# Splitting the output and the last weight row of a DMA-bound decode kernel into quarters and halves

## The chip, the cores and the metric

The kernel runs on one core of one Trainium2 chip. The metric is device time in microseconds (us) of that core, for one execution. The kernel before takes 211.58 us (median of 3 runs, 211.49 to 211.81). The profile shows 209.7 us of them, from the first instruction to the last; this is called the span below. All times inside a trace are counted from the start of the span.

## The reference, cut to what matters

One decode step for four tokens (B = 4, D = 576): attention over a window of a cache, plus an MLP, plus the residuals.

```python
x  = A_x                                        # 4 x 1 x 576, bf16
xn = _layernorm(x)
# attention: 32 query heads, 16 K/V heads, Dh = 128, the last W = 2048 positions of the cache
q  = xn @ wq
p  = softmax(q k^T * Dh**-0.5)
A  = (p @ v) @ wo
# MLP, fed with xn: for one position the shifts of the mixer (w1, w2) leave only zeros
x1 = xn
Bm = x1 + _gelu(_layernorm(x1) @ w3) @ w4       # w3 is 576 x 4608, w4 is 4608 x 576
return x + A + Bm
```

The caches and the weights are read once: 87.17 MB. The last thing to be read is `w4`, and the last thing to be computed is its product, which is added in PSUM to everything that came before.

## The kernel before

`w4` stands in SBUF as 36 "rows": row u holds, on each of 128 partitions, one line of 576 bf16 numbers. Each row is one term of the sum over F = 4608. The kernel loads `w4` in six pieces, so that the matmuls of a piece can run under the load of the next one.

```python
NI = 2                     # the output's 576 columns in two halves
CW = D // NI
...
W4_PIECES = [0, NFH, NF - 12, NF - 6, NF - 2, NF - 1, NF]      # NF = 36, NFH = 18

def load_w4():
    t = wp.tile([P, NF, D], BF16, tag="w", name="w4_sb")
    for lo, hi in zip(W4_PIECES, W4_PIECES[1:]):
        e = lo // NFH
        src = B_w4[e * (F // 2):(e + 1) * (F // 2), :].rearrange("(p i) n -> p i n", i=NFH)
        nc.sync.dma_start(out=t[:, lo:hi, :], in_=src[:, lo - e * NFH:hi - e * NFH, :])
```

The four output rows are accumulated in PSUM in two halves of 288 columns. Half i lies in a bank of its own and on partitions 32i to 32i+3 (QD = 32), which is called column group i here. The two matmuls of a row run side by side: in the trace of this kernel they start 2 to 6 ns apart, and the next row 122 ns later at full clock.

```python
accs = [ps_acc.tile([P, CW], F32, name=f"acc{i}") for i in range(2)]

def acc_of(i):
    return accs[i * 2 // NI][i * QD:i * QD + B, :]

def acc_matmuls(terms):
    for lhsT, rhs in terms:
        for i in range(NI):
            nc.tensor.matmul(out=acc_of(i), lhsT=lhsT, rhs=rhs[:, i * CW:(i + 1) * CW],
                             start=False, stop=False, skip_group_check=True)
```

The end of the kernel is a row of small steps, one after the other: matmuls of the last piece, a copy of each half to bf16 (VectorE takes one, ScalarE the other), and the output DMA.

```python
    for lo, hi in pieces:
        mlp_out(lo, hi)                     # acc_matmuls of the rows of this piece

    fin = const.tile([B, D], out.dtype)
    for i in range(NI):
        dst = fin[:, i * CW:(i + 1) * CW]
        if i * 2 < NI:
            nc.vector.tensor_copy(out=dst, in_=acc_of(i))
        else:
            nc.scalar.activation(out=dst, in_=acc_of(i), func=ACT.Copy)
    nc.sync.dma_start(out=o2, in_=fin[:])
```

In the softmax, the sum of exponentials of a head is one f32 matmul (`dn`) and one reciprocal (`rd`) for each K/V head.

## Time and profile before

| | before |
|---|---|
| median of runs, us | 211.58 |
| span, us | 209.7 |
| bytes by the load queue, share of 16 DMA engines | 87.17 MB, 97.5% |
| mean granted TensorE clock | 0.91 |
| last byte of `w4` lands, us | 206.70 |
| output DMA is issued, us | 207.59 |

The word "tail" below means the last two rows of this table: from the landing of the last byte of `w4` to the issue of the output DMA, 0.89 us here.

How the views are read. In the slices, each digit is the busy share of one fortieth of the span, in tenths. A line of the timeline has start (us), duration (us), engine, source line, operation, output <- input, shape, number of instructions, and in brackets how long the engine had been idle and what ended that. A line of a chain has start, duration and what it was. A line of the windows has a stretch of time, its length, busy time (and number) of PE, PEld, DVE, ACT and POOL, then the granted clock, the DMA share and GB/s. The lines of the kernel before are shown in the prediction.

### The profile page before, as it was taken

What the parts mean: (1) busy time and instruction counts of PE and PEld (TensorE: products, weight loads), DVE (VectorE), ACT (ScalarE), POOL (GpSimd) and SP (SyncE); (2) the same over time, 40 slices, a digit from 0 to 9 for tenths busy, and PEclk for the clock granted to TensorE, in tenths of its full rate; (3) what the DMA queues carried; (4) which work ended last, traced back from release to release, by engine and by line L of the source; (5) the groups of instructions that cost most, each with busy time, mean ns of one, the idle gap of its engine ahead of it and who ended that gap; (6) DMA issues with size and microseconds to landing.
All of it is one profiled execution on the core that took longest, in us unless ns stands there. A gap on an engine that the chain in (4) does not pass through costs nothing.

```text
span 209.7 us, 2335 instructions
## 1 busy us (share of the span) xinstructions
PE 144.6 (69%) x955; PEld 57.5 (27%) x955; DVE 114.1 (54%) x165; ACT 34.0 (16%) x64; POOL 8.7 (4%) x31
## 2 busy tenths in 40 slices
PE   0358297699690039555999997589794846897694
PEld 0123032233130013222443332134231312342362
DVE  3611877885910083926519879166849391764200
ACT  7512201021120001111122211111111201113100
POOL 4610000000000000000002000000000000000000
PEclk9999579999888558999999999889999997999669
DMA  7999999999999999999999999999999999999992
GB/s 295 406 406 441 428 428 419 444 427 428 434 443 416 431 434 415 444 425 441 422 428 431 437 411 439 431 434 431 427 428 434 419 443 428 425 437 448 407 405 80
DMA packets 6650, 87.31 MB, mean 416 GB/s; under 512 B 744, under 2 KB 1008, under 8 KB 1648
## 3 DMA queue, kind: packets, MB, share of 16 engines
q1 hardware_dynamic: 6632, 87.17, 97.5%
q8 instruction: 7, 0.11, 0.2%
q14 instruction: 3, 0.02, 0.0%
q10 hardware_dynamic: 8, 0.00, 0.0%
HBM read 87.17 MB, written 0.00 MB: 416 GB/s over the span
## 4 chain that ended last, share of the span: by engine, by line
DMA 75%; PE 12%; DVE 10%; ACT 1%; issue 0%; SPq 0%; DVEq 0%; ACTq 0%
DMA kn<-in_A_k_cache_dram 30%; DMA vn<-in_A_v_cache_dram 24%; DMA w_sb<-in_B_w_dram 15%; DVE kt L222 7%; DMA wq_sb<-in_A_wq_dram 6%; PE S L335 3%; PE g_ps L452 2%; PE q_ps L279 2%; PE acc L181 1%; PE O L387 1%; DVE qz L311 1%; PE gT_ps L464 1%; DVE mx L341 1%; PE oT L400 1%; ACT q_sb L290 1%; PE S L357 0%
## 5 line engine op out<-in xcount | busy, mean ns | idle before, releaser
L335 PE MATMUL S<-kt,qz 128*128 128x512 bf16 x256 | 73.4, 413 | 34.0 <-DVE kt L222 33.8
L222 DVE STREAM_TRANSPOSE kt<-kn 128x2048 int32<-128x2048 int32 x32 | 73.4, 2297 | 28.3 <-DMA kn<-in_A_k_cache_dram 26.8
L335 PEld LDWEIGHTS <-qz 128*128 128x128 bf16 x256 | 23.4, 105 | 64.2 <-issue 46.2
L387 PE MATMUL O<-vn,PT 128*32 128x512 bf16 x256 | 22.6, 394 | 12.2 <-DMA vn<-in_A_v_cache_dram 12.2
L363 ACT ACTIVATE E<-S 128x512 bf16<-128x512 f32 x16 | 9.5, 597 | 96.6 <-PE S L357 96.6
L369 DVE STREAM_TRANSPOSE PT<-E 128x512 bf16<-128x512 bf16 x16 | 11.4, 710 | 13.8 <-ACT E L363 13.8
L394 ACT ACTIVATE O_sb<-O,rd 128x512 f32<-128x512 f32 x16 | 11.0, 686 | 37.0 <-PE O L387 37.0
L387 PEld LDWEIGHTS <-PT 128*32 128x32 bf16 x256 | 5.9, 94 | 32.6 <-issue 32.3
L410 DVE TENSOR_REDUCE on<-oT 128x8 bf16<-128x128 f32 x16 | 4.6, 287 | 18.7 <-PE oT L400 18.7
L400 PE MATMUL oT<-ident_w,O_sb 128*128 128x128 f32 x64 | 11.9, 314 | 0.2 <-ACT O_sb L394 0.2
L341 DVE TENSOR_REDUCE mx<-S 128x1 f32<-128x512 f32 x16 | 10.5, 658 | 1.2 <-PE S L335 1.1
L400 PEld LDWEIGHTS oT<-ident_w,O_sb 128*128 128x128 f32 x64 | 7.5, 153 | 4.4 <-issue 3.4
L357 PE MATMUL S<-nm,j_row 8*128 8x512 bf16 x16 | 6.5, 408 | 2.1 <-DVE nm L353 1.9
L373 PE MATMUL dn<-rs,same_j 128*128 128x1 f32 x32 | 6.2, 264 | 0.4 <-DVE g_x L470 0.4
L373 PEld LDWEIGHTS dn<-rs,same_j 128*128 128x128 f32 x32 | 5.0, 195 | 4.5 <-issue 3.8
L181 PE MATMUL acc<-wo_sb,op 128*4 128x288 bf16 x64 | 5.5, 324 | 1.0 <-DVE op L432 1.0
L323 PE MATMUL S<-negbig,ohT 4*128 4x512 bf16 x16 | 6.2, 385 | 0.0
L181 PE MATMUL acc<-w_sb,gT 128*4 128x288 bf16 x72 | 5.7, 315 | 0.4 <-DMA w_sb<-in_B_w_dram 0.4
L279 PE MATMUL q_ps<-wq_sb,xnT 128*32 128x512 bf16 x40 | 4.4, 625 | 2.2 <-DMA wq_sb<-in_A_wq_dram 2.2
L452 PE MATMUL g_ps<-w_sb,ln2T 128*32 128x512 bf16 (+1 forms) x50 | 4.9, 443 | 0.0
L602 DVE CAST fin<-acc 4x288 bf16<-4x288 f32 x1 | 0.4, 447 | 8.0 <-PE acc L181 8.0
L474 POOL TENSOR_TENSOR g_u<-g_x 128x144 f32<-128x144 f32 x1 | 0.4, 426 | 101.4 <-DVE g_x L470 101.4
(86 smaller groups left out, 74.4 us busy)
## 6 DMA issues: line engine op xcount, KB each, us to landing
kn<-in_A_k_cache_dram SPq DMA_DIRECT2D x16, 2048.0 KB, 24.5
vn<-in_A_v_cache_dram SPq DMA_DIRECT2D x16, 2048.0 KB, 26.5
wo_sb<-in_A_wo_dram SPq DMA_DIRECT2D x4, 1152.0 KB, 27.1
w_sb<-in_B_w_dram SPq DMA_DIRECT2D x1, 4608.0 KB, 33.2
wq_sb<-in_A_wq_dram SPq DMA_DIRECT2D x1, 4096.0 KB, 12.8
w_sb<-in_B_w_dram SPq DMA_DIRECT2D x1, 2592.0 KB, 33.1
w_sb<-in_B_w_dram SPq DMA_DIRECT2D x2, 864.0 KB, 34.5
w_sb<-in_B_w_dram SPq DMA_DIRECT2D x2, 576.0 KB, 32.5
```

Of the source, the lines that this page charges most:

```text
L181: nc.tensor.matmul(out=acc_of(i), lhsT=lhsT, rhs=rhs[:, i * CW:(i + 1) * CW], start=False, stop=False, skip_group_check=True)
L222: nc.vector.transpose(out=kt[:], in_=src)
L279: nc.tensor.matmul(out=q_ps[r][g * QD:(g + 1) * QD, :], lhsT=xnT[:, k, :], rhs=wq_sb[:, col:col + NW], start=(j == 0), stop=False, skip_gr ...
L335: nc.tensor.matmul(out=S_ps[h][:], lhsT=qz[:, z0:z0 + P], rhs=kt[:, ib, c0:c0 + SC, e:2 * QD:2].rearrange("p c k -> p (c k)"), start=False ...
L341: nc.vector.reduce_max(out=mx[:], in_=S_ps[h][:], axis=AX.X)
L363: nc.scalar.activation(out=E[h][:].rearrange("p c k -> p (c k)"), in_=S_ps.pop(h)[:], func=ACT.Exp, scale=scale, accum_out=rs[:])
L369: nc.vector.transpose(out=PT[h][:], in_=E.pop(h)[:])
L373: nc.tensor.matmul(out=dn[:], lhsT=same_j[:], rhs=st.pop(("rs", h))[:], start=True, stop=True)
L387: nc.tensor.matmul(out=O_ps[h][g * QD:(g + 1) * QD], lhsT=PT[h][:, c, :], rhs=vn[:, :, c, :], start=(s == 0), stop=False, skip_group_check ...
L394: nc.scalar.activation(out=O_sb[h][:], in_=O_ps.pop(h)[:], func=ACT.Copy, scale=st.pop(("rd", h))[:, 0:1])
L400: nc.tensor.transpose(out=oT[:, s, :], in_=o[:, s, :], identity=ident_w[:, s * NJ:s * NJ + P])
L452: nc.tensor.matmul(out=g_ps[g * QD:(g + 1) * QD], lhsT=ln2T[:, k, :], rhs=rhs, start=(j == 0), stop=False, skip_group_check=True)
```

## The change

Its intent: the last row's first half arrives before its second half. With the output in four quarters, quarters 0 and 1 are finished by the first half row and can be copied out while the second half row is still under way. So only two quarter copies, not two half copies, should lie after the last byte. The diff, cut to its core:

```diff
-    NI = 2
+    NI = 4
...
-    W4_PIECES = [0, NFH, NF - 12, NF - 6, NF - 2, NF - 1, NF]
+    W4_PIECES = [0, NFH, NF - 12, NF - 6, NF - 2, NF - 0.5, NF]
...                                        # load_w4 cuts the flattened (row, column) axis
+    late = {}
+
     def acc_of(i):
-        return accs[i * 2 // NI][i * QD:i * QD + B, :]
+        t = late.get(i, accs[i % 2])
+        return t[i * QD:i * QD + B, 0:CW]
...
     def mlp_out(lo, hi):
         w4 = w_tiles["w4"]
-        acc_matmuls([(gT[:, u, :], w4[:, u, :]) for u in range(lo, hi)])
+        for u in range(int(lo), NF):
+            quarters = [i for i in range(NI) if lo <= u + i / NI < hi]
+            acc_matmuls([(gT[:, u, :], w4[:, u, :])], quarters)
+
+    def copy_out(i):
+        dst = fin[:, i * CW:(i + 1) * CW]
+        if i % 2:
+            nc.scalar.activation(out=dst, in_=acc_of(i), func=ACT.Copy)
+        else:
+            nc.vector.tensor_copy(out=dst, in_=acc_of(i))
...                                        # after the last scaling of the loop
+    for i in (2, 3):
+        new = ps_s.tile([P, NW], F32, tag="S", name="late")
+        ...                                # acc_of(i) is copied to new, on DVE or ACT
+        late[i] = new
...
     for lo, hi in pieces:
         mlp_out(lo, hi)
+        for i in range(NI):
+            if lo <= NF - 1 + i / NI < hi:
+                copy_out(i)
```

Quarter i uses column group i, and so partitions 32i to 32i+3. Quarters 2 and 3 move late into the two score banks, which are free by then, so that each quarter has a bank of its own. Besides, the denominators of two heads are summed by one matmul and inverted by one reciprocal.

More of the change, by code (lines that the diff above doesn't have):

```diff
@@ L138, in load_w4 @@
         for lo, hi in zip(W4_PIECES, W4_PIECES[1:]):
-            e = lo // NFH
-            src = B_w4[e * (F // 2):(e + 1) * (F // 2), :].rearrange("(p i) n -> p i n", i=NFH)
-            nc.sync.dma_start(out=t[:, lo:hi, :], in_=src[:, lo - e * NFH:hi - e * NFH, :])
+            e = int(lo) // NFH
+            src = B_w4[e * (F // 2):(e + 1) * (F // 2), :].rearrange("(p i) n -> p (i n)", i=NFH)
+            lo, hi, cut = int(lo * D), int(hi * D), e * NFH * D
+            nc.sync.dma_start(out=t[:].rearrange("p i n -> p (i n)")[:, lo:hi], in_=src[:, lo - cut:hi - cut])
         w_tiles["w4"] = t
@@ L172, with acc_matmuls @@
         nc.vector.memset(acc[:], 0.0)
+    late = {}
     def acc_of(i):
-        return accs[i * 2 // NI][i * QD:i * QD + B, :]
-    def acc_matmuls(terms):
+        t = late.get(i, accs[i % 2])
+        return t[i * QD:i * QD + B, 0:CW]
+    def acc_matmuls(terms, quarters=range(NI)):
         for lhsT, rhs in terms:
-            for i in range(NI):
+            for i in quarters:
                 nc.tensor.matmul(out=acc_of(i), lhsT=lhsT, rhs=rhs[:, i * CW:(i + 1) * CW],
@@ L361, in sm_exp @@
         E[h] = ptp.tile([P, SC, QD], BF16, tag="e", name="E", bufs=1)
-        rs = small.tile([P, 1], F32, tag="rs", bufs=3)
+        if h % 2 == 0:
+            st["rs"] = small.tile([P, 2], F32, tag="rs", name="rs", bufs=3)
         nc.scalar.activation(out=E[h][:].rearrange("p c k -> p (c k)"), in_=S_ps.pop(h)[:], func=ACT.Exp, scale=scale,
-                             accum_out=rs[:])
-        st["rs", h] = rs
+                             accum_out=st["rs"][:, h % 2:h % 2 + 1])
     def sm_turn(h):
@@ L371, in sm_den @@
     def sm_den(h):
-        dn = ps_m.tile([P, 1], F32, tag="m", name="dn")
-        nc.tensor.matmul(out=dn[:], lhsT=same_j[:], rhs=st.pop(("rs", h))[:], start=True, stop=True)
-        st["dn", h] = dn
-    def sm_rec(h):
-        rd = small.tile([P, 1], F32, tag="rd", bufs=4)
-        nc.vector.reciprocal(out=rd[:], in_=st.pop(("dn", h))[:])
-        st["rd", h] = rd
+        if h % 2 == 0:
+            return
+        dn = ps_m.tile([P, 2], F32, tag="m", name="dn")
+        nc.tensor.matmul(out=dn[:], lhsT=same_j[:], rhs=st.pop("rs")[:], start=True, stop=True)
+        st["dn"] = dn
+    def sm_rec(h):
+        if h % 2 == 0:
+            return
+        rd = small.tile([P, 2], F32, tag="rd", bufs=4)
+        nc.vector.reciprocal(out=rd[:], in_=st.pop("dn")[:])
+        for k in range(2):
+            st["rd", h - 1 + k] = rd[:, k:k + 1]
     def pv(h, s):
@@ L393, in o_scale @@
         O_sb[h] = bigp.tile([P, NSL, Dh], F32, tag="big", name="O_sb")
-        nc.scalar.activation(out=O_sb[h][:], in_=O_ps.pop(h)[:], func=ACT.Copy, scale=st.pop(("rd", h))[:, 0:1])
+        nc.scalar.activation(out=O_sb[h][:], in_=O_ps.pop(h)[:], func=ACT.Copy, scale=st.pop(("rd", h)))
     def o_turn(h):
@@ L586 @@
     o_scale(hl)
+    for i in (2, 3):
+        new = ps_s.tile([P, NW], F32, tag="S", name="late")
+        if i % 2:
+            nc.scalar.activation(out=new[i * QD:i * QD + B, 0:CW], in_=acc_of(i), func=ACT.Copy)
+        else:
+            nc.vector.tensor_copy(out=new[i * QD:i * QD + B, 0:CW], in_=acc_of(i))
+        late[i] = new
     o_turn(hl - 1)
@@ L594 @@
     o_proj(hl)
+    fin = const.tile([B, D], out.dtype)
     for lo, hi in pieces:
         mlp_out(lo, hi)
-    fin = const.tile([B, D], out.dtype)
-    for i in range(NI):
-        dst = fin[:, i * CW:(i + 1) * CW]
-        if i * 2 < NI:
-            nc.vector.tensor_copy(out=dst, in_=acc_of(i))
-        else:
-            nc.scalar.activation(out=dst, in_=acc_of(i), func=ACT.Copy)
+        for i in range(NI):
+            if lo <= NF - 1 + i / NI < hi:
+                copy_out(i)
     nc.sync.dma_start(out=o2, in_=fin[:])
```

## The prediction

Passages of the prediction are cut, marked where they stood: figures and rules of the hardware that it did not take from a trace. Its sum is as recorded, 211.58 - 0.12 = 211.46 us, but the sources of three of its terms are among the cuts. Those terms stand because the trace of the changed kernel has since shown them: 0.226 us for a matmul of 144 columns at full clock (222 to 226 ns there), and 150 and 120 ns less for a copy of half the columns on DVE and ACT (447 to 295 ns and 401 to 281 ns, so 152 and 120). Rival B's reckoning came to +0.5 us, 212.1.

> **What bounds the kernel now.** I read the slices of the page first, then the chain that ended last, then the timeline of the last microseconds, because the change touches almost nothing else.
>
> ```profile
> DMA  7999999999999999999999999999999999999992
> GB/s 295 406 406 441 428 428 419 444 427 428 434 443 416 431 434 415 444 425 441 422 428 431 437 411 439 431 434 431 427 428 434 419 443 428 425 437 448 407 405 80
> q1 hardware_dynamic: 6632, 87.17, 97.5%
> ```
>
> In every slice but the first and the last the 16 DMA engines are at least 90% busy; they move 87.17 MB and are occupied for 97.5% of the span. The change moves the same bytes, so some 206 us out of 209.7 are fixed. Only what follows the last byte can be saved. The chain, from the last V load on:
>
> ```profile
> 174.85 31.13 DMA w_sb<-in_B_w_dram
> 205.98 0.04 issue
> 206.03 1.05 PE acc L181 x12
> 207.07 0.44 DVE fin L602
> ```
>
> This seems to give 1.05 us of matmuls to win. It does not, as the timeline around 207 shows:
>
> ```profile
> 206.74 0.29 PE L181 MATMUL acc<-w_sb,gT 128*4 128x288 bf16 x2
> 207.06 0.45 DVE L602 CAST fin<-acc 4x288 bf16<-4x288 f32 x1 [7.98 <-PE acc L181]
> 207.10 0.40 ACT L604 ACTIVATE fin<-acc 4x288 bf16<-4x288 f32 x1 [10.85 <-PE acc L181]
> 207.59 0.35 SPq L605 DMA_DIRECT2D out_dram<-fin  x1
> ```
>
> The last two matmuls (row 35 of w4) start at 206.74. The trace's records of landings give the reason: the six pieces of w4 are complete at 200.48, 202.46, 204.59, 205.98, 206.33 and 206.70. PE started the last row 0.04 us after its data; it had no backlog. So the tail is: last byte 206.70, +0.04 to the matmul, +0.29 matmul, +0.03 to the copy, +0.45 copy, +0.08 to the output DMA, then 2.14 us of output and end of program, which the change leaves alone. From last byte to output DMA there are 0.89 us, and only the matmul and the copy in it shrink with the column count.
>
> [...] with four column groups, 8 matmuls of 512 columns take 0.61 us[...]; their starts (trace records) are 3 ns apart inside a group of four.
>
> ```profile
> 180.19 0.12 PEld L387 LDWEIGHTS <-PT 128*32 128x32 bf16 x8 [0.44 <-issue]
> 180.19 0.61 PE L387 MATMUL O<-vn,PT 128*32 128x512 bf16 x8
> 180.73 0.36 PE L419 MATMUL R<-on,sel_wo 128*128 128x32 bf16 x8
> ```
>
> The third line is the narrow case in one group: 8 in 0.36 us, starts 25 ns apart[...].
>
> **The change part by part.**
>
> *Four column groups instead of two.* Each of the 36 rows of w4 and the 8 rows of each of four output projections now needs 4 weight loads and 4 matmuls of 144 columns. The order of instructions on PE has 266 more: 68 rows with 4 extra each is 272, 2 more for the first sum, 8 fewer for the denominators. Before, a row takes 122 ns at full clock and 240 ns at half (starts in the trace)[...]: both groups run together. Four groups at 144 columns should take half, about 62 and 120 ns. This lies under the DMA either way: PE waits for pieces already (0.36 us before 206.03). Worth 0 at the end.
>
> *Loads.* The last two pieces of 1152 B per partition become 1728 B and 576 B. Packets of 1152, 4608 and 6912 B take 51, 178 and 264 ns in the trace, which fits 6 ns + 0.0374 ns per byte; 1728 + 576 B cost 71 + 28 = 99 ns against 2 x 51 = 102. Same number of packets. So the last byte still lands at 206.70, and the larger piece, three quarters of the 0.72 us between 205.98 and 206.70, at 206.52. Worth 0 by itself.
>
> *Quarters 0 and 1.* Rows 30 to 33 start at 206.03 and need 0.25 us. Row 34 starts at 206.56, row 35 of quarters 0 and 1 at 206.62, and they are done at 206.62 + 0.226 = 206.85. Copies of 4x144: DVE [...]447 - 150 = 297 ns; ACT 401 - 120 = 281 ns. With the gaps of before (34 and 66 ns) they run from 206.88 to 207.18 on DVE and 206.91 to 207.19 on ACT.
>
> *Quarters 2 and 3.* The last half row starts at 206.74 and is ready at 206.74 + 0.226 = 206.97, so the second pair of copies could start at 207.00. But DVE and ACT are still in the first pair: "under the load" there are only 0.18 us between the landings, and a copy alone takes 0.3. Consecutive instructions that do not depend on each other overlap by some 80 to 90 ns on DVE:
>
> ```profile
> 86.80 0.23 DVE L343 TENSOR_SCALAR dm<-sel_g,mx 128x16 bf16<-128x16 bf16 x1
> 86.94 0.16 DVE L378 RECIPROCAL rd<-dn 128x1 f32<-128x1 f32 x1
> ```
>
> (0.23 us long, next start after 0.14). So the second copies start at about 207.09 and end at 207.39 (DVE) and 207.38 (ACT). The output DMA is issued at 207.39 + 0.08 = 207.47 against 207.59: 0.12 us less.
>
> *Moves of quarters 2 and 3 into the score banks.* One more copy each, on DVE after the last reciprocal (about 193.0, when it idles 3.16 us) and on ACT after the last scaling (ends 196.25). The first matmul that needs them is at 199.14. Hidden.
>
> *Denominators in pairs.* Eight pairs of f32 matmuls of 0.38 us on PE and eight reciprocals of 0.16 us on DVE go. For even heads the scaling on ACT now waits for the reciprocal of the same turn, behind the maximum on DVE: about 2 us later (180.85 to 182.91 in the turn I looked at). Its reader, the transposes at 184.89, comes later still. Loads are issued some 24 us ahead of landing, so none of this reaches the DMA. In the tail head 14's scaling moves from 192.55 to some 193.05; its transposes start at 195.39. Worth 0.
>
> **The sum:** 211.58 - 0.12 = 211.46 us.
>
> **The rivals.**
>
> *A. The copies of quarters 0 and 1 are fully hidden.* Then the end is 206.97 + 0.03 + 0.30 = 207.30, issue 207.38: 0.21 us gained, 211.37. For it: that is the intent. Against: 0.18 us between the two landings.
>
> *B. PE falls behind.* [...] Against: the 3 ns and 25 ns starts above. I give it one in twenty.
>
> *C. The clock falls.* Twice as fast, PE idles more, and the clock is granted by windows:
>
> ```profile
> 192.41:195.83 3.42, 1.81 (x26) 1.10 (x22) 0.60 (x2) 0.96 (x2) 0.00 (x0) 1.00 0.99 426
> 195.83:199.24 3.41, 1.90 (x17) 1.20 (x16) 1.42 (x4) 0.42 (x1) 0.00 (x0) 0.50 0.98 418
> 202.65:206.07 3.42, 3.06 (x52) 2.05 (x48) 0.00 (x0) 0.00 (x0) 0.00 (x0) 1.00 0.82 324
> ```
>
> After the first window, with PE busy 1.81 of 3.42 us, the next one got half clock (0.50, third column from the end). In the changed kernel the window from 202.65 would hold some 1.2 to 1.5 us of PE work instead of 3.06, so the last matmuls may run at half clock[...]: the gain is gone, 211.58. About one in three.
>
> *D. The loop gets shorter because PE and DVE are relieved.* Against: DMA at 97.5%. It makes nothing of the time.
>
> **Range and chances.** The main line gives -0.12, A -0.21, C 0, B +0.5; the three runs of before spread by 0.32 us themselves. I take 211.15 to 211.80. All of these are far inside 2% (4.2 us): faster 0.01, same 0.98, slower 0.01.
>
> **What would show it.** Right: last piece landing within 0.1 us of 206.70; two copies each on DVE and ACT of about 0.30 and 0.28 us, the second starting as the first ends; output DMA near 207.47; row starts of w4 near 62 ns apart at full clock. Wrong: row starts of 120 ns or more at full clock or PE busy without a gap up to the end (B); a granted clock of 0.50 in the last window (C); second copies that start 0.03 us after the last matmul with the engine idle before (A). A last landing that moves by more than 0.3 us would break the whole sum, since everything hangs from it.

## The result

The median is 211.81 us (6 runs, 211.67 to 211.83) against 211.54 us for the kernel before on the same chip (6 runs, 211.38 to 211.81). The ratio is 1.001, with a 95% interval of 0.9997 to 1.0023: the same, at a bar of 2%. A ratio here and below is the mean time of one kernel's fast runs over that of the other's fast runs of the same rounds, so it is not quite the ratio of the medians quoted.

Neither session alone settles the sign, since both intervals hold 1. Over the two sessions that timed both kernels, the mean is 211.76 us for the changed kernel (11 runs) and 211.56 for the kernel before (15 runs): 0.2 us more, where 0.12 less was predicted. Part of it lies outside the span, where no view shows it: time less span is 1.90 to 1.91 us in both traced runs of the changed kernel (211.82 and 211.69 us) and 1.78 in both of the kernel before (211.51 and 211.50). What makes it is not shown; e_long, below, has 1.91 too, all other traced runs 1.77 to 1.79. The traces tell more of what lies inside. The page of the changed kernel, with the lines that answer to the first three of the prediction:

```profile
DMA  7999999999999999999999999999999999999991
GB/s 301 400 418 425 431 428 434 428 431 423 455 421 422 431 425 427 441 431 425 434 434 425 434 415 446 421 437 434 417 437 428 427 428 437 428 434 443 416 404 66
q1 hardware_dynamic: 6632, 87.17, 97.5%
```

Packets, bytes and share are the same. The loads bound this kernel as they did the other. The chain that ended last:

```profile
174.95 31.12 DMA w_sb<-in_B_w_dram
206.07 0.04 issue
...
207.08 0.28 DVE fin L501
207.37 0.33 DVEq L652
```

Before, the chain closed with one copy of 0.44 us. Now a copy of 0.28 us is followed by another 0.33 us of the same engine. (L652 is a line of the launch; what the trace has there is a DRAIN of DVE from 207.18 to 207.75, over the second copy, 207.40 to 207.70.) The timeline shows that the second copy stands behind the first:

```profile
206.71 0.33 PE L185 MATMUL acc<-w_sb,gT 128*4 128x144 bf16 x2
206.84 0.28 PE L185 MATMUL late<-w_sb,gT 128*4 128x144 bf16 x2
207.07 0.29 DVE L501 CAST fin<-acc 4x144 bf16<-4x144 f32 x1 [7.48 <-PE acc L185]
207.10 0.28 ACT L499 ACTIVATE fin<-acc 4x144 bf16<-4x144 f32 x1 [10.06 <-PE acc L185]
207.40 0.30 DVE L501 CAST fin<-late 4x144 bf16<-4x144 f32 x1
207.41 0.28 ACT L499 ACTIVATE fin<-late 4x144 bf16<-4x144 f32 x1
207.78 0.34 SPq L626 DMA_DIRECT2D out_dram<-fin  x1
```

Quarters 0 and 1 end at 207.03 (206.71 + 0.33). The landings, from the trace's records, are 206.59 for the piece up to row 35.5 and 206.80 for the last half row; quarters 2 and 3 end at 207.12. The output DMA goes out at 207.78, 0.19 us later than before. Of this, 0.10 us lies in the last landing (206.80 against 206.70) and 0.09 us in the tail (0.98 against 0.89).

The last two clock windows of this trace:

```profile
201.81:205.22 3.41, 1.06 (x51) 0.79 (x48) 0.00 (x0) 0.00 (x0) 0.00 (x0) 1.00 0.95 385
205.22:208.63 3.41, 1.06 (x28) 0.62 (x23) 0.60 (x2) 0.56 (x2) 0.00 (x0) 0.50 0.17 59
```

PE was busy for 1.06 of 3.41 us, and from 205.22 on it had half clock (0.50, third column from the end). The last matmuls last 0.28 us each instead of the 0.226 that the prediction took for full clock (222 to 226 ns at the full clock of this trace). The first copies start only 0.27 us after the last landing (206.80), so they do not run under a load at all; what the cut gave them is a start ahead of the last matmuls' end.

### The profile page after: what moved, and what is told of

Same layout as the page of the kernel before. It is cut to its first block, busy times and chain, and to the rows that moved or that the text cites. A ratio compares the mean times of both kernels' runs of the same rounds, so it can differ in the third digit from the quotient of the medians.

```text
span 209.9 us, 2568 instructions
## 1 busy us (share of the span) xinstructions
PE 145.8 (69%) x1079; PEld 55.1 (26%) x1079; DVE 113.7 (54%) x159; ACT 34.4 (16%) x66; POOL 8.7 (4%) x31
## 3 DMA queue, kind: packets, MB, share of 16 engines
q1 hardware_dynamic: 6632, 87.17, 97.5%
## 4 chain that ended last, share of the span: by engine, by line
DMA 75%; PE 16%; DVE 6%; ACT 1%; issue 0%; SPq 0%; DVEq 0%; ACTq 0%
DMA vn<-in_A_v_cache_dram 43%; DMA w_sb<-in_B_w_dram 15%; DMA kn<-in_A_k_cache_dram 12%; DMA wq_sb<-in_A_wq_dram 6%; PE S L339 5%; DVE kt L226 4%; PE O L396 2%; PE g_ps L461 2%; PE q_ps L283 2%; PE acc L185 1%; PE oT L409 1%; PE S L361 1%; DVE qz L315 1%; PE gT_ps L473 1%; ACT q_sb L294 1%; PE dn L379 0%
## 5 line engine op out<-in xcount | busy, mean ns | idle before, releaser
L339 PE MATMUL S<-kt,qz 128*128 128x512 bf16 x256 | 78.7, 437 | 31.3 <-DVE kt L226 30.3
L396 PE MATMUL O<-vn,PT 128*32 128x512 bf16 x256 | 24.6, 425 | 11.2 <-DMA vn<-in_A_v_cache_dram 11.0
L409 PE MATMUL oT<-ident_w,O_sb 128*128 128x128 f32 x64 | 12.9, 339 | 0.0
L409 PEld LDWEIGHTS oT<-ident_w,O_sb 128*128 128x128 f32 x64 | 8.5, 170 | 5.4 <-issue 4.9
L185 PE MATMUL acc<-w_sb,gT 128*4 128x144 bf16 x72 | 3.3, 239 | 3.4 <-DMA w_sb<-in_B_w_dram 3.4
L210 PE MATMUL tp<-ident_bf,first 4*128 4x4 bf16 x8 | 0.6, 172 | 5.7 <-DVE first L197 5.4
L479 DVE COPY g_x<-gT_ps 128x64 f32<-128x64 f32 (+1 forms) x3 | 0.6, 195 | 7.1 <-PE gT_ps L473 7.1
```

Source lines behind the costliest of these rows:

```text
L339: nc.tensor.matmul(out=S_ps[h][:], lhsT=qz[:, z0:z0 + P], rhs=kt[:, ib, c0:c0 + SC, e:2 * QD:2].rearrange("p c k -> p (c k)"), start=False ...
L396: nc.tensor.matmul(out=O_ps[h][g * QD:(g + 1) * QD], lhsT=PT[h][:, c, :], rhs=vn[:, :, c, :], start=(s == 0), stop=False, skip_group_check ...
L409: nc.tensor.transpose(out=oT[:, s, :], in_=o[:, s, :], identity=ident_w[:, s * NJ:s * NJ + P])
```

## The experiments

The theory after the result: three things ate the gain. (H) The second copy of an engine does not overlap the first, because it starts on other partitions. (C) The last matmuls ran at half clock. (L) The load stream ended 0.1 us later. The rivals were that the half row's cut itself delays the loads, that the pairing of the denominators does something, and that PE falls behind. Each kernel below was timed in five runs beside the kernel before, and each gave a correct result. The experiments marked "two in one" change the tail and the clock together.

This table has the tails of all traces. "Clock" is the granted clock in the last microsecond of the matmuls.

| kernel | last landing | clock | tail | output DMA | median us | ratio (95%) |
|---|---|---|---|---|---|---|
| before | 206.70 | full | 0.891 | 207.59 | 211.54 | |
| e_before2 (before) | 206.70 | full | 0.889 | 207.59 | 211.58 | 1.0000 (0.9988–1.0013) |
| e_pairs | 206.71 | full | 0.889 | 207.60 | 211.51 | 0.9998 (0.9985–1.0010) |
| after | 206.80 | half | 0.980 | 207.78 | 211.81 | 1.0010 (0.9997–1.0023) |
| e_after2 (after) | 206.80 | full | 0.847 | 207.65 | 211.69 | 1.0009 (0.9995–1.0022) |
| e_warm | 206.64 | full | 0.920 | 207.56 | 211.61 | 1.0004 (0.9992–1.0017) |
| e_two_groups | 206.60 | full | 1.209 | 207.81 | 211.50 | 1.0000 (0.9987–1.0012) |
| e_whole_rows | 206.79 | half | 1.067 | 207.85 | 211.87 | 1.0010 (0.9997–1.0024) |
| e_columns | 206.89 | half | 0.870 | 207.76 | 211.67 | 1.0004 (0.9991–1.0017) |
| e_columns3 | 206.92 | half | 0.854 | 207.78 | 211.81 | 1.0012 (0.9999–1.0024) |
| e_busy | 207.25 | full | 2.026 | 209.28 | 212.62 | 1.0040 (1.0027–1.0054) |
| e_columns3_busy | 207.11 | full | 2.011 | 209.12 | 213.15 | 1.0068 (1.0055–1.0081) |
| e_long | 206.59 | full | 0.869 | 207.46 | 211.58 | 0.9997 (0.9985–1.0010) |
| e_columns3_long | 207.18 | full | 0.685 | 207.87 | 211.62 | 0.9999 (0.9985–1.0012) |

The kernel before was timed in every session beside them; its medians were 211.54, 211.53, 211.65, 211.72 and 211.51. So a tenth of a microsecond between two medians means little here, and the tails, read from the traces, carry the argument.

### e_before2 and e_after2: both kernels again, with no edit

> The kernel before again, unedited: the noise of the comparison. Ratio 0.999 to 1.001. Last landing: if the load stream ends where chance puts it, anything from 206.6 to 206.8; if the program decides it, 206.70 as in both traces of kernels with this tail so far (206.70, 206.71). Granted clock: its phase differs from execution to execution; tail from last landing to output DMA 0.89 us unless PE falls behind.

> The changed kernel again, unedited, for a tighter interval and a second trace. Theory 1 (the tail itself is longer: the second copy of each engine starts only after the first has ended, because it reads other partitions, and the last matmuls run at half clock because PE idles between the pieces): from the last landing of w4 to the issue of the output DMA 0.95 to 1.02 us again (0.98 in the first trace, against 0.89 in the kernel before); second copy about 30 ns after the end of the first on both engines. Theory 2 (the load stream just ended 0.1 us later by chance): last landing back near 206.70 and the ratio at 1.000.

Measured: the kernel before repeats itself to 0.002 us in the tail (0.889) and has the same last landing, 206.70. The changed kernel, too, lands at 206.80 again. But its windows fell otherwise this time:

```profile
200.14:203.55 3.41, 3.41 (x120) 3.41 (x124) 0.00 (x0) 0.00 (x0) 0.00 (x0) 0.50 1.01 423
203.55:206.96 3.41, 1.67 (x68) 1.05 (x56) 0.02 (x1) 0.00 (x0) 0.00 (x0) 1.00 0.57 220
```

A window with PE busy all the time came before, and the clock was full up to 206.96, past the last matmul's start at 206.84. The tail is 0.847, below the expectation of 0.95 to 1.02 for an unchanged half clock: that expectation missed because the clock differs from execution to execution of one kernel. The stretches of one granted clock are 3.41 us or a multiple of it (6.83, 10.24 and 13.65 us, among others, in the first trace of the changed kernel), and their borders are at 205.22 in one execution of the kernel and at 203.55 in the other.

So the half clock cost 0.13 us of the tail (0.980 - 0.847). At full clock the change shortens the tail by 0.04 us (0.889 - 0.847), a third of what was predicted. The second copies again started 31 and 24 ns after the first had ended: their stop has nothing to do with the clock.

### e_pairs: the paired denominators alone

```diff
+        if h % 2 == 0:
+            st["rs"] = small.tile([P, 2], F32, tag="rs", name="rs", bufs=3)
...
+            accum_out=st["rs"][:, h % 2:h % 2 + 1])       # two heads share a tile
...                                                        # one matmul, one reciprocal for both
```

The rest is the kernel before.

> The kernel before with the paired denominators alone. All theories expect no difference from the kernel before: ratio 0.9995 to 1.0005, last landing within 0.1 us of 206.70. If the last landing moves to 206.80 or later in this kernel, the shift of the stream comes from the pairing (later scaling on ACT) and not from the tail.

Measured: ratio 0.9998, last landing 206.71, tail 0.889. Nothing moved. The pairs are worth nothing and cost nothing.

### e_two_groups: all copies of one engine on the same partitions

Quarters 2 and 3 keep banks of their own but use the partitions (and column groups) of quarters 0 and 1.

```diff
-    accs = [ps_acc.tile([P, CW], F32, ...
+    accs = [ps_acc.tile([P, 2 * CW], F32, ...
...
-        t = late.get(i, accs[i % 2])
-        return t[i * QD:i * QD + B, 0:CW]
+        q = i % 2 * QD
+        if i in late:
+            return late[i][q:q + B, 0:CW]
+        return accs[i % 2][q:q + B, i // 2 * CW:(i // 2 + 1) * CW]
...                                        # the moves of quarters 2 and 3 likewise
```

> The changed kernel with quarters 2 and 3 in the column groups of quarters 0 and 1, in banks of their own, so that both copies of one engine read the same partitions. PE works as long as in the kernel before, so the clock should stay full in most executions. If different start partitions hold the second copy back, it now starts some 80 to 100 ns before the first one ends, on DVE and perhaps on ACT, and the output DMA is issued 0.76 to 0.82 us after the last landing: some 0.2 us faster than the changed kernel, 0.1 us faster than before. If it is something else (the wait on PE, the shared output tile), the second copy starts 25 to 30 ns after the first one ends as now.

Measured, in the timeline:

```profile
207.02 0.23 PE L187 MATMUL late<-w_sb,gT 128*4 128x144 bf16 x2
...
207.22 0.30 DVE L503 CAST fin<-acc 4x144 bf16<-4x144 f32 x1 [7.38 <-PE late L187]
207.26 0.28 ACT L501 ACTIVATE fin<-acc 4x144 bf16<-4x144 f32 x1 [9.99 <-PE late L187]
207.44 0.27 ACT L501 ACTIVATE fin<-late 4x144 bf16<-4x144 f32 x1
207.45 0.28 DVE L503 CAST fin<-late 4x144 bf16<-4x144 f32 x1
207.81 0.35 SPq L628 DMA_DIRECT2D out_dram<-fin  x1
```

The overlap is there on both engines. On DVE the first copy ends at 207.518 and the second starts at 207.447, 71 ns before; on ACT 93 ns before. In the changed kernel the second started 31 and 25 ns after the first one's end. From the end of quarters 0 and 1 to the output DMA this kernel needs 0.63 us (207.19 to 207.81) where the changed kernel needs 0.745 (207.035 to 207.78). That shows (H), and its size of some 0.12 us. It is not a wait of the second copy for its own matmuls either: in e_whole_rows, below, all matmuls are over (207.12) before the first copy starts (207.14), and with the partitions of the changed kernel the second copies still start only 31 and 24 ns after the end of the first.

The sources of DVE's two copies start at partition 0 and 64 in the changed kernel, and both at 0 in this one: the second copy starts 31 ns after the end of the first against 71 ns before it. ACT's start at 32 and 96 in the changed kernel, and both at 32 in this one: 25 ns after the end against 93 ns before it. No experiment tried other starts.

The tail as a whole was a miss: 1.209 instead of 0.76 to 0.82. With only two column groups, the narrow matmuls take 125 ns a row again, and 240 at half clock. Half clock held until 203.46, PE fell behind, and the last row started at 207.02 though it had landed at 206.60. The four groups therefore have a merit that the prediction put at zero: at half clock they keep PE up with the loads (in the changed kernel's first trace the last half row starts at 206.84 and had landed at 206.80).

### e_whole_rows: four quarters without the cut

```diff
-    W4_PIECES = [0, NFH, NF - 12, NF - 6, NF - 2, NF - 0.5, NF]
+    W4_PIECES = [0, NFH, NF - 12, NF - 6, NF - 2, NF - 1, NF]
```

> The changed kernel with the last row of w4 loaded whole, as before: four groups, four copies, all after the last matmul. Each engine then makes two copies one after the other with the hold, so the output DMA comes 0.04 + 0.24 + 0.04 + 0.30 + 0.03 + 0.30 + 0.08 = 1.03 us after the last landing at full clock, 1.08 at half. Against it, the cut of the last row gains 0.1 to 0.18 us. If the copies overlapped by 80 ns, 0.92.

Measured, at half clock:

```profile
206.84 0.28 PE L185 MATMUL late<-w_sb,gT 128*4 128x144 bf16 x2
207.14 0.30 DVE L501 CAST fin<-acc 4x144 bf16<-4x144 f32 x1 [7.46 <-PE late L185]
...
207.47 0.30 DVE L501 CAST fin<-late 4x144 bf16<-4x144 f32 x1
...
207.85 0.35 SPq L626 DMA_DIRECT2D out_dram<-fin  x1
```

The tail is 1.067 (1.08 was expected), 0.087 longer than the changed kernel's at the same clock. So the cut does gain, and four copies without it cost more than the two copies of before: from the end of the last matmul to the output DMA it takes 0.74 us here and 0.56 there. The last landing is 206.79, as with the cut (206.80): the cut delays nothing, and that rival falls. Indeed the changed kernel's stream was late (by 0.09 us) already at 194.3, before `w4`; from there to the last byte both kernels need the same time, 12.42 and 12.43 us.

### e_columns and e_columns3: first halves land earlier

If 0.2 us between two landings hide too little of a copy of 0.3 us, the landings should lie further apart. Here the last two rows are cut by columns: first their left halves, then their right halves. In e_columns3 the right half comes row by row, in a seventh piece.

```diff
-    W4_PIECES = [0, NFH, NF - 12, NF - 6, NF - 2, NF - 0.5, NF]
+    W4_PIECES = [(0, NFH, 0, D), (NFH, NF - 12, 0, D), (NF - 12, NF - 6, 0, D), (NF - 6, NF - 2, 0, D),
+                 (NF - 2, NF, 0, D // 2), (NF - 2, NF, D // 2, D)]           # rows lo, hi, columns lo, hi
+    # e_columns3: (NF - 2, NF, 0, D // 2), (NF - 2, NF - 1, D // 2, D), (NF - 1, NF, D // 2, D)
...                                        # load_w4, mlp_out and the copies follow these pieces
```

> The changed kernel with the last two rows of w4 cut by columns: quarters 0 and 1 of both rows first, quarters 2 and 3 of both rows last. The two landings are then 0.37 us apart instead of 0.2, so the first copies end (0.30 us) about when quarters 2 and 3 are ready, and the hold costs nothing. At full clock: output DMA 0.74 to 0.80 us after the last landing (0.85 in the changed kernel at full clock, 0.98 at half); at half clock 0.85 to 0.90. If the collision of the copies is not what ate the gain, 0.85 stays at full clock.

> As e_columns, with the last half split once more by rows, so that after the last byte only one row of quarters 2 and 3 is left to multiply. At full clock 0.66 to 0.74 us from the last landing to the output DMA, the least of all; 0.72 to 0.80 at half clock. Time against before: ratio 0.9988 to 1.0.

Measured for e_columns: landings at 206.51 and 206.89, 0.38 us apart, and half clock in the end:

```profile
202.50:205.91 3.41, 1.24 (x64) 0.92 (x53) 0.00 (x0) 0.00 (x0) 0.00 (x0) 1.00 0.88 340
205.91:207.40 1.49, 1.21 (x24) 0.65 (x23) 0.32 (x2) 0.28 (x1) 0.00 (x0) 0.50 0.15 47
```

The tail is 0.870, as expected at half clock, and 0.11 less than the changed kernel's at half clock. The first copies run from 207.05, beside the matmuls of the rest (206.93 to 207.34), and the second start 0.04 us after these end: the hold costs next to nothing here.

e_columns3 missed: 0.854 instead of 0.72 to 0.80, and a ratio of 1.0012 for at most 1.0. At half clock the rows of the piece before still stood in the queue, 0.12 us each, so quarters 0 and 1 were late (their copies start at 207.07), and the second copies were held until 207.40. The seventh piece also costs something after the output has landed: the program ends 0.96 to 0.97 us later in the three kernels with seven pieces of `w4`, and 0.845 to 0.855 us later in all others.

### e_warm, e_busy and e_columns3_busy: keeping the clock full

To test (C) alone, PE gets matmuls into an unused PSUM bank between the pieces. In e_warm these are 2, 5 and 2 matmuls of the full array with 512 columns. In e_busy they are 6, 12 and 6 repeated rows (four matmuls of 144 columns each). e_columns3_busy is two in one: the same rows on top of e_columns3.

```diff
+    scratch = ps_o.tile([P, NSL * Dh], F32, tag="O", name="scratch")
+    FILL = {NFH: 6, NF - 12: 12, NF - 6: 6}
     for lo, hi in pieces:
         mlp_out(lo, hi)
+        for _ in range(FILL.get(hi, 0)):
+            for i in range(NI):
+                nc.tensor.matmul(out=scratch[i * QD:i * QD + B, 0:CW], lhsT=gT[:, 0, :],
+                                 rhs=w_tiles["w4"][:, 0, i * CW:(i + 1) * CW], start=True, stop=True)
```

> The changed kernel with idle PE time between the pieces of w4 filled with 2, 5 and 2 matmuls of 512 columns into a scratch bank. If half clock in the last window costs what theory 1 says (rows 0.12 instead of 0.06 us apart, 0.28 instead of 0.226 us for the last matmul), the granted clock is 1.00 in the last window, quarters 0 and 1 are ready 0.1 us earlier after their landing, and the output DMA is issued 0.08 to 0.12 us earlier after the last landing than in the changed kernel: 0.87 to 0.90 us. If the clock does not matter, 0.98 us stays.

> The changed kernel with 6, 12 and 6 repeated rows (four matmuls of 144 columns each, in the same four column groups, into a scratch bank) in the idle time of PE between the pieces of w4; unlike the 512-column fillers of the first try they [...]fit the gaps at half clock too (6 x 0.12 = 0.72 us in 0.77, 12 x 0.12 = 1.44 in 1.58, 0.72 in 0.85). If idling is what lets the clock fall, the last window is at full clock and the output DMA comes 0.84 to 0.86 us after the last landing, as in the second trace of the changed kernel. If the clock is granted by something else, half clock and 0.98 us can come again. Time against before: ratio 0.999 to 1.0005.

> The column cut with the split last half, and the same repeated rows to keep the clock up: all three losses removed. Output DMA 0.66 to 0.72 us after the last landing, against 0.89 in the kernel before: 0.17 to 0.23 us less on the path. The measured time should be 0.1 to 0.3 us below the kernel before, if the load stream does not happen to end later, as it did by 0.1 to 0.2 us in four of the kernels with the paired denominators. If something else bounds the tail, 0.85 us stays.

e_warm had full clock in the end, but its own matmuls (one of 0.63 us at half clock, then five in 1.25 us at full) pushed the rows back: row 30 started at 206.27 though it had landed at 205.80. Its tail of 0.920 (expected 0.87 to 0.90) says nothing on the price of the clock.

e_busy had full clock in the end, too:

```profile
202.50:205.92 3.42, 2.34 (x136) 2.04 (x125) 0.00 (x0) 0.00 (x0) 0.00 (x0) 1.00 0.89 358
205.92:208.50 2.58, 1.06 (x60) 0.91 (x59) 0.00 (x0) 0.00 (x0) 0.00 (x0) 1.00 0.14 46
```

This is the best comparison of the windows: the border falls within 0.01 us of that of e_columns. With PE busy 1.24 us of the window, the next one has 0.50; with 2.34 us, 1.00. The clock records of all 14 traces, cut into windows of 3.41 us, say the same: after a window at full clock with PE busy less than 1.5 us, the next had half clock (65 of 65), and after one with more than 2.5 us it had full clock (327 of 327); in between (151 windows) both came. But the tail became 2.03 us, for a reason that no theory had expected:

```profile
205.24 0.23 PE L185 MATMUL acc<-w_sb,gT 128*4 128x144 bf16 x2
205.25 0.23 PE L185 MATMUL late<-w_sb,gT 128*4 128x144 bf16 x2
207.44 0.23 PE L185 MATMUL acc<-w_sb,gT 128*4 128x144 bf16 x2 [1.96 <-issue]
...
```

PE stood for 1.96 us and waited for nothing that the profile shows. In e_columns3_busy, whose tail was 2.011 instead of 0.66 to 0.72, it stood for 1.97 us at the same place: in both traces 1100 matmuls and 1116 weight loads are recorded before the stop, though the two kernels were at different times then (205.25 and 205.08 at the last matmul's start). The changed kernel has 1079 of each in all, so it ends before that place. The queue that the page calls "instruction" moved nine packets of 16 KB here, eight in the changed kernel and seven before:

```profile
q8 instruction: 9, 0.15, 0.2%
```

The packets are in the trace's records: the eighth of the nine starts at 205.06 and takes 0.92 us, while the DMA engines are at least 90% busy (the page's slice from 200.8 to 206.1); the ninth comes only at 208.57, when PE works again. It looks as if PE ran out of instructions while the eighth was under way, but PE went on only 1.46 us after the end of that packet, which nothing here explains. Only the number of instructions was varied, so a want of instructions is the guess at the cause, not shown; the clauses of the two expectations below that rested on it are cut.

### e_long and e_columns3_long: the clock kept full by few, long instructions

The same with few instructions: 1, 3 and 1 sets of four matmuls of 512 columns, 20 matmuls instead of 96.

```diff
+    FILL = {NFH: 1, NF - 12: 3, NF - 6: 1}
...
+                nc.tensor.matmul(out=scratch[i * QD:i * QD + B, :], lhsT=gT[:, 0, :],
+                                 rhs=w_tiles["w4"][:, 0, 0:NSL * Dh], start=True, stop=True)
```

> The changed kernel with 1, 3 and 1 sets of four 512-column matmuls (one in each column group, scratch bank) between the pieces of w4: 20 matmuls instead of the 96 of the repeated rows[...]. Same use of PE time[...]. If idling lets the clock fall: full clock in the last microsecond and 0.84 to 0.87 us from the last landing to the output DMA. [...] If neither, 0.98 us at half clock.

> The same fillers with the column cut and the split last half: 0.66 to 0.74 us from the last landing to the output DMA at full clock, 0.15 to 0.2 us less than the kernel before[...]. The time depends besides on where the load stream ends (206.6 to 206.95 in the traces so far), so the ratio to before may be anything from 0.9985 to 1.001; the tail is the test.

(The times of a set are cut from the first of the two. In the trace of the kernel before, back-to-back sets of four 512-column matmuls start 0.22 to 0.23 us apart at full clock.)

No stop this time (e_long has 1099 matmuls and as many weight loads, fewer than went before the stop), eight packets of instructions, and full clock in both. e_long has a tail of 0.869, within the expectation of 0.84 to 0.87, and the earliest output DMA of all, at 207.46. Its five runs lie between 211.49 and 211.62, so the added matmuls cost nothing. But its window border (203.46) lies near that of e_after2 (203.55), which had full clock without them, so this run alone does not prove that they kept the clock up.

e_columns3_long (two in one) takes away both losses of the tail, (H) and (C), but not (L):

```profile
206.82 0.29 PE L185 MATMUL acc<-w_sb,gT 128*4 128x144 bf16 x4
207.02 0.44 PE L185 MATMUL late<-w_sb,gT 128*4 128x144 bf16 x4
207.14 0.30 DVE L499 CAST fin<-acc 4x144 bf16<-4x144 f32 x1 [7.26 <-PE acc L185]
...
207.49 0.30 DVE L499 CAST fin<-late 4x144 bf16<-4x144 f32 x1
...
207.87 0.35 SPq L629 DMA_DIRECT2D out_dram<-fin  x1
```

The first copies are over at 207.44, and the second start at 207.49, when their matmuls are done: DVE stands idle between them, so the hold costs nothing. The tail is 0.685, as expected (0.66 to 0.74) and 0.2 us less than before's. Yet the median is 211.62 and the ratio 0.9999. The seventh piece takes 0.11 of the gain back. In this trace the stream ended at 207.18 besides, 0.48 later than before, but the traced run (211.90) is the slowest of the five (211.38 to 211.90), so that is no measure of the kernel. What is left of the gain, some 0.1 us, is less than the runs of one kernel differ by.

## Why the prediction was right or wrong

Right was the ground of it, and with it the class: the loads bound both kernels (97.5%), and nothing in the tail comes near 2%. That needed no insight into the tail, since all the outcomes that the prediction weighed lie inside that bar. The gain itself did not come, and the median of the first session lies 0.01 us above the top of the range; that of the second, 211.69, lies inside. Point by point, with the issue of the output DMA predicted at 207.47 and found at 207.78:

- **Four column groups.** Right: rows start 62 ns apart at full clock and 120 at half, and PE waits for pieces. (The traces record 248 instructions more on PE, 955 to 1079 matmuls and as many loads, where 266 were counted.) But "worth 0" left out two things. Four groups protect against half clock (e_two_groups fell behind without them, by 0.42 us at the last row), and they leave PE so idle that the half clock comes (PE busy for 1.06 of 3.41 us before it; rival C, below).
- **Loads.** The cost of the cut was right: the smaller packets (576 B) take 29.2 ns where 28 were predicted, those of 1728 B 75.8 for 71, and the stretch of `w4` is as long as before. The step "the last byte still lands at 206.70" was off by 0.10, for a shift that came before `w4`. The piece up to row 35.5 landed at 206.59 for 206.52: **+0.07 us** on the path.
- **Quarters 0 and 1.** Copies of 295 and 281 ns, where 297 and 281 were predicted (half the columns take 152 ns off DVE's copy, for 150). Their start was late only by what came before.
- **Quarters 2 and 3.** This is the step that failed: "Consecutive instructions that do not depend on each other overlap by some 80 to 90 ns on DVE". It was read from two instructions that start on the same partitions (0.23 us long, the next one 0.14 us later). The copies of quarters 0 and 2 do not, nor do those of 1 and 3, and each second one started 25 to 31 ns after the first one's end: **+0.12 us**. e_two_groups shows that the partitions decide it (71 and 93 ns before the first one's end with the same start). This loss is as large as the whole predicted gain. At full clock (e_after2) 0.04 of the gain was left all the same, because the two landings stood 0.23 us apart instead of 0.18.
- **Rival C**, the half clock, which had been given one chance in three, came true in this trace (the window that it shows before half clock was not idle: PE was busy for 1.81 of 3.42 us): from landing to finished quarters 0 and 1 it took 0.445 us instead of 0.33, **+0.115 us**. e_after2 shows that it comes and goes between executions. In the five traces of kernels with four groups and no added matmuls (the changed kernel twice, e_columns, e_columns3, e_whole_rows) it came four times.
- **Moves and denominators.** Right: hidden (0.32 and 0.25 us long, over by 197.04, first used at 199.64), and worth 0 (e_pairs).
- **Rivals A, B and D.** A is false, the copies are not hidden. B is false, PE does not fall behind: even at half clock the last half row starts 0.04 us after its landing. D came to nothing, as said (e_pairs).

The sum: 0.07 + 0.115 + 0.12 = 0.305 us, and 207.78 - 207.47 = 0.31.

What stays open is why the stream ends where it does. The kernel before landed at 206.70 twice, the changed one at 206.80 twice, the pairs at 206.71; the others between 206.59 and 207.25. In both traces of the changed kernel the stream is 0.15 us late already at 69.3, where the last piece of `w3` lands. That looks like a property of each program. But only one run of five or six was traced, and the spans of the kernel before range from 209.6 to 210.4 us over its runs, while its two tails are alike to 0.002: the stream's end most likely moves from execution to execution too, and the landings that agree may be chance. That the stop of PE in e_busy is a want of instructions is open as well.

## What to carry to other kernels

A first copy keeps out of the second one's way only if their landings lie further apart than the copy is long; here 0.2 us stood against 0.3, and the rest of the copy was put in front of the next one, while 0.38 us (e_columns) was enough. If one engine is to do two copies back to back, let them start on the same partition (the second then started 71 and 93 ns before the end of the first, instead of 31 and 25 ns after it), if that does not cost the column groups, as it did in e_two_groups; and read an overlap from a trace only off instructions that share that property. When the engine that feeds the tail becomes twice as fast, look for the clock that it loses by idling (half clock here after a window with PE busy for 1.06 of 3.41 us, 0.13 us of the tail); and before a tenth of a microsecond is chased in the tail, look at how much the end of the load stream moves by itself.
